# Half-height rows of a projection joined to a row-split matmul run, with the moves that go with it

## Chip, cores, metric

One core of one Trainium2 chip. The metric is the device time of one execution in microseconds, as the median of several runs; the profile gives the span of one execution, which is some 2 us shorter. Every profiled run told of here was in the fast state, with a granted TensorE clock of 0.998 or more, and the ratios use fast runs alone.

Abbreviations of the profile: PE is TensorE, DVE is VectorE, ACT is ScalarE, POOL is GpSimd, SPq is the queue of SyncE, which issues the DMAs here.

## The reference, cut to what matters

```python
# x: 1 x 2048 x 576, 32 heads of 18; feed-forward width 4608
h = layernorm(x) * (1 + ca) + sa
x = x + ga * (linear_attention(h) @ wo)          # the output projection
h = layernorm(x) * (1 + cb) + sb
x = x + gb * (relu(h @ w1) @ w2)                 # first and second feed-forward product
```

## The kernel before

The rows are 16 tiles of 128. After a first phase (keys, values, queries of all tiles, and tiles 0 and 1 up to the feed-forward input) come eight blocks. Block b does the feed-forward part of tiles 2b and 2b+1 and, in between, attention, projection and second layer norm of the next two tiles. The first product of a block (`l1`) has three groups; 576 is 4 x 128 + 64, so the last 64 rows are done as a pair of half-height matmuls, one in rows 0 to 63 of the array and one in rows 64 to 127, each in its own bank:

```python
def l1_rest(js, u, hb):
    for n, j in enumerate(js):
        for hf in range(2):
            b0 = 64 * hf
            pe.matmul(PS[:, 2 * u + hf, n * 256:n * 256 + 256], lhsT=w1b[b0:b0 + 64, j * P:(j + 1) * P],
                      rhs=hb[b0:b0 + 64, 4, :], start=False, stop=False, skip_group_check=True)
```

The output projection has the same 64 rows left, but does them as a full-array matmul with zeros:

```python
def wo_mm(t, pr, add_x):
    for k in range(2):
        if add_x:      # tiles 0 and 1: residual through an identity matmul
            pe.matmul(pr[:, k, 0:HD], lhsT=ident[:, 0:P], rhs=x_sb[:, t, k * HD:(k + 1) * HD], start=True, stop=False)
        for ci in range(NC):                        # NC = 5, the fifth is half empty
            pe.matmul(pr[:, k, 0:HD], lhsT=oT[:, t % 2, ci, :], rhs=wo_sb[:, ci, k * HD:(k + 1) * HD], ...)
```

What is called here as each block runs (shortened):

```python
def in_l1(g, u):                                    # during the first product
    if (g, u) in ((0, -1), (0, 1)):  q_fin(q); q_in(q + NL)      # query preparation of the next two tiles
    if (g, u) in ((1, 2), (2, 1)):   num_mm(t, pr); num_o(t, pr); turn_dma(oT[:, t % 2], o_sb[:, t % 2, :])
def in_l2(pos):                                     # during the second product, 14 positions of 9 matmuls
    if pos in (1, 4):  wo_mm(t, pr, False); <residual add>; bn(1, t)
    if pos in (2, 6):  ln2_rs(t); ln2_apply(t, None); turn_dma(h2...)
    if pos == 12:                                   # scale the normalised rows of both tiles, in place
        for ci in range(NC):
            dve.tensor_scalar(out=hb[:, ci, :], in0=hb[:, ci, :], scalar1=..., scalar2=..., op0=ALU.mult, op1=ALU.add)
```

Query preparation is a VectorE sum and reciprocal, a GpSimd multiply of 128 x 576 (L291), a transposing DMA, and a reload of the same buffer for a later tile, which must wait until that transpose has landed.

The softmax here doesn't subtract the row's maximum and nothing guards it: scores larger than these inputs give would overflow.

## Time and profile before

| | before |
|---|---|
| time | 393.02 us (391.85 to 393.25) |
| span, TensorE busy | 390.7 us, 98% |
| first phase, up to the first feed-forward matmul | 93.5 us |
| one block (blocks 0 to 6) | 37.05 us |
| block 7 and tail | 37.8 us |

The block lengths are distances between the starts of two first products in the timeline of TensorE, for instance 315.82 - 278.77. The view of waits shows none of TensorE in the blocks, so a block is all but the sum of its matmuls (a wait of 0.09 us that the view doesn't show comes up in experiment 7).

### The profile page before, as it was taken

How to read it: one execution, taken by the hardware profiler on the slowest of the kernel's cores; microseconds unless marked ns; L12 is line 12 of the kernel's file. 1: busy time of each engine (PE TensorE's matmuls, PEld its weight loads, DVE VectorE, ACT ScalarE, POOL GpSimd, SP SyncE). 2: the span in 40 equal slices, each digit the busy share in tenths (PEclk: the TensorE clock that was granted, in tenths of full speed). 3: DMA queues.
4: the chain of work that ended last, by engine and by line, in shares of the span. 5: the costliest groups of instructions: out<-in, count | busy, mean ns of one | idle time of the engine just before them, and what ended most of it. 6: DMA issues, size and time to landing. Idle time of an engine off the chain costs nothing.

```text
span 390.7 us, 8908 instructions
## 1 busy us (share of the span) xinstructions
PE 383.8 (98%) x3693; PEld 311.7 (80%) x3693; DVE 244.3 (63%) x452; ACT 157.9 (40%) x360; POOL 142.3 (36%) x199
## 2 busy tenths in 40 slices
PE   8999999999999999999999999999999999999995
PEld 4778888878887888788888878887888788878874
DVE  0889998854879746573755567458555664653221
ACT  1798779699531233124213510531143123312510
POOL 2155858741101510740164045306510641072045
PEclk9999999999999999999999999999999999999999
DMA  7999739795732151125313311450143124010001
GB/s 291 418 420 403 274 133 354 178 306 161 189 65 35 47 121 20 35 61 109 35 27 83 80 35 32 107 65 19 47 93 35 24 69 51 18 34 33 3 0 32
DMA packets 49515, 44.36 MB, mean 114 GB/s; under 512 B 39361, under 2 KB 42050, under 8 KB 48706
## 3 DMA queue, kind: packets, MB, share of 16 engines
q1 hardware_dynamic: 49186, 43.59, 39.6%
q8 instruction: 29, 0.48, 0.5%
q10 hardware_dynamic: 288, 0.19, 0.2%
q14 instruction: 12, 0.10, 0.1%
HBM read 27.97 MB, written 6.49 MB: 88 GB/s over the span
## 4 chain that ended last, share of the span: by engine, by line
PE 86%; POOL 6%; ACT 2%; DVE 2%; DMA 2%; issue 1%; SPq 0%; POOLq 0%; DVEq 0%; ACTq 0%
PE PS L683 33%; PE PS L742 29%; PE PS L274 9%; PE PS L410 5%; PE PS L690 5%; POOL wo_sb L637 2%; PE PS L235 2%; PE PS L391 1%; ACT RT L279 1%; POOL RH L754 1%; DMA gatd<-gt 1%; PE PS L324 1%; POOL RT L291 1%; DMA ga_row<-gatd 1%; DVE st L240 1%
## 5 line engine op out<-in xcount | busy, mean ns | idle before, releaser
L683 PE MATMUL PS<-h,R 128*128 128x256 bf16 x1152 | 133.5, 273 | 0.0
L683 PEld LDWEIGHTS <-R 128*128 128x128 bf16 x1152 | 109.8, 98 | 17.5 <-issue 5.1
L742 PEld LDWEIGHTS <-RH 128*128 128x128 f16 x864 | 84.5, 98 | 21.8
L728 POOL TENSOR_TENSOR yt<-yt,gb_row 128x288 f32<-128x288 f32 x23 | 16.8, 731 | 167.0 <-DVE yt L727 167.0
L742 PE MATMUL PS<-R,RH 128*128 128x288 bf16 (+1 forms) x576 | 75.6, 286 | 0.0
L697 ACT ACTIVATE RH<-PS 128x256 f16<-128x256 f32 x72 | 27.7, 384 | 114.0 <-PE PS L690 107.4
L699 DVE SCALAR_TENSOR_TENSOR RH<-PS,RH 128x256 f16<-128x256 f32 x72 | 30.1, 419 | 68.2 <-ACT RH L697 68.2
L279 ACT ACTIVATE RT<-PS,rs 128x576 bf16<-128x576 f32 x64 | 43.0, 750 | 7.5 <-PE PS L274 7.1
L698 ACT ACTIVATE RH<-PS 128x512 f16<-128x512 f32 x72 | 42.9, 595 | 7.8 <-PE PS L683 6.5
L746 ACT ACTIVATE RS<-PS 128x288 f32<-128x288 f32 x24 | 9.9, 411 | 75.9 <-PE PS L742 75.9
L742 PE MATMUL PS<-RT,RH 128*128 128x288 f16 x288 | 37.9, 286 | 0.0
L274 PE MATMUL PS<-RH,R 116*128 116x288 bf16 x240 | 31.8, 286 | 0.5 <-ACT RH L631 0.5
L754 POOL TENSOR_TENSOR RH<-RH,RT 128x2304 f16<-128x2304 f16 x7 | 31.8, 4548 | 0.0
L274 PE MATMUL PS<-RH,RT 116*128 116x288 bf16 x240 | 31.7, 286 | 0.0
L274 PEld LDWEIGHTS <-R 116*128 116x128 bf16 x240 | 22.9, 98 | 6.4 <-issue 0.7
L274 PEld LDWEIGHTS <-RT 116*128 116x128 bf16 x240 | 22.7, 98 | 5.5
L420 DVE TENSOR_SCALAR xn<-x_sb,mv,rs 128x576 bf16<-128x576 bf16 (+1 forms) x28 | 22.4, 842 | 7.3 <-ACT rs L415 7.3
L729 POOL TENSOR_TENSOR x_sb<-yt,x_sb 128x288 bf16<-128x288 f32 x31 | 22.8, 737 | 5.9 <-DVE yt L725 4.1
L240 DVE BATCH_NORM_STATS2 st<-x_sb 128x6 f32<-128x288 bf16 x60 | 24.2, 445 | 0.5
L410 PE MATMUL PS<-wo_sb,oT 128*128 128x288 bf16 x160 | 22.6, 286 | 0.2 <-POOL wo_sb L637 0.2
L284 DVE TENSOR_REDUCE Rk<-RT 128x64 f32<-128x1152 bf16 x16 | 21.2, 1332 | 1.4 <-ACT RT L279 1.4
L284 DVE TENSOR_REDUCE Rq<-RT 128x64 f32<-128x1152 bf16 x16 | 21.5, 1342 | 0.0
(115 smaller groups left out, 414.2 us busy)
## 6 DMA issues: line engine op xcount, KB each, us to landing
R<-in_w1a_dram SPq DMA_DIRECT2D x4, 1152.0 KB
eqd<-RT SPq DMA_DIRECT2D x14, 288.0 KB, 5.8
RT<-eqd SPq DMA_DIRECT2D x14, 288.0 KB, 2.7
R<-in_w2a_dram SPq DMA_DIRECT2D x3, 864.0 KB, 10.4
R<-in_w2b_dram SPq DMA_DIRECT2D x2, 1296.0 KB, 10.9
out_dram<-x_sb SPq DMA_DIRECT2D x15, 144.0 KB, 3.3
RT<-in_xT_dram SPq DMA_DIRECT2D x2, 640.0 KB
x_sb<-in_xk_dram SPq DMA_DIRECT2D x3, 288.0 KB
```

The source lines that it names most:

```text
L240: dve.bn_stats(out=s[:, hf, :], in_=x_sb[:, t, hf * HD:(hf + 1) * HD])
L274: pe.matmul(pr[:, k, 0:HD], lhsT=xt(t, ck), rhs=w[0:R, ck, k * HD:(k + 1) * HD], start=(ck == 0), stop=(ck == NC - 1))
L279: act.activation(out=E.rearrange("p (b h s e) -> p b h s e", b=2, s=2, e=DH)[:, :, :, s, :], in_=pr[:, :, 0:HD].rearrange("p b (h e) -> p ...
L284: dve.tensor_reduce(out=Rr, in_=E.rearrange("p (c e) -> p c e", e=DH), axis=AXX, op=ALU.add)
L410: pe.matmul(pr[:, k, 0:HD], lhsT=oT[:, t % 2, ci, :], rhs=wo_sb[:, ci, k * HD:(k + 1) * HD], start=(ci == 0 and not add_x), stop=(ci == NC ...
L683: pe.matmul(PS[:, 2 * u + hf, n * 256:n * 256 + 256], lhsT=w1a[:, ci, jj * P:(jj + 1) * P], rhs=hb[:, ci, :], start=(n == 0 and ci == 0), ...
L697: act.activation(out=A11[:, j, :], in_=lo[:, :, 0, :], func=ACT.Relu)
L698: act.activation(out=A2[:, j, :, :], in_=PS[:, 2 * u + 1, :].rearrange("p (n s f) -> p n s f", n=2, s=2), func=ACT.Relu)
L699: dve.scalar_tensor_tensor(out=U3[:, j, :], in0=lo[:, :, 1, :], scalar=0.0, in1=A11[:, j, :], op0=ALU.max, op1=ALU.subtract)
L729: pool.tensor_tensor(out=x_sb[:, t, c], in0=y, in1=x_sb[:, t, c], op=ALU.add)
L742: pe.matmul(PS[:, bank, 0:HD], lhsT=am[:, j, :], rhs=bm[:, j, :], start=first and j == 0, stop=(j % 9 == 8), skip_group_check=True)
L754: pool.tensor_tensor(out=A12, in0=A12, in1=U2, op=ALU.subtract)
```

## The change

The intent: TensorE is the bound, so take matmul time from it. From tile 6 on, the last 64 rows of the projection become a pair of half-height matmuls that joins an existing row-split run. For that the projection moves into the first product, attention ahead of it, and the query preparation back into the second product. Both halves of the array need the 64 rows, so the weights hold them twice and ScalarE copies 64 columns before the transpose (neither is in the cut diff). For tiles 0 and 1 VectorE adds the residual in place of four identity matmuls. The very last product is cut in two column halves in two banks, so that VectorE's work on the first half lies beside the second.

```diff
 # first phase, order of jobs (W projection, lb/lr/ap statistics, logarithm and exponential, scaling; eQ exponentials)
-Q9:1 eQ8 W0:3 eQ9 sq7 lb0 ot1:2 sq8 Q10:0 oc1 sq6 lr0 W1:1 ap0 eQ10 sq9 lb1 xc0 ht0:2 ...
+Q9:1 eQ8 W0:3 eQ9 sq7 xr0 lb0 ot1:2 sq8 Q10:0 oc1 sq6 lr0 W1:1 ap0 eQ10 sq9 xr1 lb1 ht0:2 ...
+    def add_res(t, pr):
+        x = v2(x_sb[:, t, :])
+        dve.tensor_tensor(out=x, in0=x, in1=pr[:, :, 0:HD], op=ALU.add)
 # [... cut: same for W, lb, ap without the identity matmul ...]
 # first product
             for u in range(3):
                 l1_rest(js[u], u, hb)
+            hooks(g, "rest")
 # blocks
+    def wo_rest(t, pr):
+        for k in range(2):
+            b0 = 64 * k
+            pe.matmul(pr[:, k, 0:HD], lhsT=oT[b0:b0 + 64, t % 2, 4, :], rhs=wo_sb[b0:b0 + 64, 4, k * HD:(k + 1) * HD],
+                      start=True, stop=False, skip_group_check=True)
+            # in_l1; blocks 0 and 1 stay much as they were [cut], and block 1 also does:
+                if b and (g, u) == (1, 0):
+                    q_next(t0 + 2)
+            # blocks 2 to 6:
+            if (g, u) in ((0, 0), (0, 2)):
+                attend(t0 + u // 2)
+            if g and u == "rest":
+                wo_rest(t0 + g - 1, pair(3))
+            if g and u == 0:
+                wo_full(t, pair(3)); add_res(t, pair(3)); bn(1, t)
+            if (g, u) == (1, 2):
+                norm2(b, t0)
+            # in_l2
+            if pos == (6 if b < 2 else 1):
+                norm2(b, t0 + 1)
+            if b > 1 and pos in (4, 9) or b == 1 and pos == 9:
+                q_next(t0 + 2 + pos // 9)
 # tail
+        for i, bank in enumerate((Z, 0)):
+            # [cut: 18 matmuls of 144 columns]
+            dve.tensor_tensor(out=yt[:, 0, c], in0=PS[:, bank, c], in1=gb_row[:, g], op=ALU.mult)
+            dve.tensor_tensor(out=x_sb[:, t, g], in0=yt[:, 0, c], in1=yl[:, c], op=ALU.add)
```

More of the change, by code (lines that the diff above doesn't have):

```diff
@@ L56 @@
 tp2 Q5:2 eQ4 sq3 tp1 wo3 nu0:3 eQ5 Q6:0 sq4 nO0 wo0 qi2 Q7:1 eQ6 wo1 sq5 ot0:2 w2b1 eQ7 nu1:3 Q8:0 nO1 oc0
-Q9:1 eQ8 W0:3 eQ9 sq7 lb0 ot1:2 sq8 Q10:0 oc1 sq6 lr0 W1:1 ap0 eQ10 sq9 lb1 xc0 ht0:2 sq10 Q11:0 ha0 hd0 lr1
-Q12:3 eQ11 ap1 Q13:2 qi3 xc1 eQ12 sq11 ht1:0 Q14:1 hd1 ha1 sq12 eQ13 Q15:3 qi4 eQ14 sq13 eQ15 sq14 sq15
+Q9:1 eQ8 W0:3 eQ9 sq7 xr0 lb0 ot1:2 sq8 Q10:0 oc1 sq6 lr0 W1:1 ap0 eQ10 sq9 xr1 lb1 ht0:2 sq10 Q11:0 ha0 hd0
+lr1 Q12:3 eQ11 ap1 Q13:2 qi3 eQ12 sq11 ht1:0 Q14:1 hd1 ha1 sq12 eQ13 Q15:3 qi4 eQ14 sq13 eQ15 sq14 sq15
 """
@@ L403, in turn_dma, with wo_mm @@
         sp.dma_start_transpose(dst, src.rearrange("p (c f) -> p c f", f=P))
-    def wo_mm(t, pr, add_x):
+    def wo_mm(t, pr):
         for k in range(2):
-            if add_x:
-                pe.matmul(pr[:, k, 0:HD], lhsT=ident[:, 0:P], rhs=x_sb[:, t, k * HD:(k + 1) * HD], start=True, stop=False)
             for ci in range(NC):
                 pe.matmul(pr[:, k, 0:HD], lhsT=oT[:, t % 2, ci, :], rhs=wo_sb[:, ci, k * HD:(k + 1) * HD],
-                          start=(ci == 0 and not add_x), stop=(ci == NC - 1))
+                          start=(ci == 0), stop=(ci == NC - 1))
+    def add_res(t, pr):
+        x = v2(x_sb[:, t, :])
+        dve.tensor_tensor(out=x, in0=x, in1=pr[:, :, 0:HD], op=ALU.add)
     def ln2_rs(t):
@@ L415, in ln2_rs, with ln2_apply @@
         act.activation(out=rs2[:, t, 0:1], in_=lnv[:, t:t + 1], func=ACT.Exp, scale=-0.5)
-    def ln2_apply(t, src):
+    def ln2_apply(t):
         def cols(o, i):
@@ L421, in cols @@
                               op0=ALU.subtract, op1=ALU.mult)
-        if src is None:
-            cols(xn[:, t % 2, 0:D], x_sb[:, t, :])
-            cols(xn[:, t % 2, D:640], x_sb[:, t, 512:D])
-        else:
-            cols(v2(xn[:, t % 2, 0:D]), src[:, :, 0:HD])
-            cols(xn[:, t % 2, D:640], src[:, 1, 224:HD])
+        cols(xn[:, t % 2, 0:D], x_sb[:, t, :])
+        cols(xn[:, t % 2, D:640], x_sb[:, t, 512:D])
     G5, FW = 504, 72
@@ L466, in tile_block @@
     SS = RS[:, 0:6 * HD].bitcast(FP32).rearrange("p (a f) -> p a f", f=HD)
+    yl = RE[:, 0:2 * HD].bitcast(FP32)
     X, Y, Z = 6, 4, 7
@@ L519, in wv_scale @@
             eng.tensor_scalar(out=o, in0=i, scalar1=f, scalar2=None, op0=ALU.mult)
-    def ln2_bn(i, pr):
-        for hf in range(2):
-            dve.bn_stats(out=st[:, i, hf, :], in_=pr[:, hf, 0:HD])
-        dve.bn_aggr(out=mv[:, 1, i, :], in_=st[:, i])
     def turn(src, pr):
@@ L642, in tile_block @@
         "oc": lambda i: act.activation(out=flat(oT[:, i]), in_=bf(at["ot", i][:, 0, :])[:, 0:640], func=ACT.Copy),
-        "W": lambda i: wo_mm(i, at["W", i], True), "lb": lambda i: ln2_bn(i, at["W", i]), "lr": ln2_rs,
-        "xc": lambda i: act.activation(out=v2(x_sb[:, i, :]), in_=at["W", i][:, :, 0:HD], func=ACT.Copy),
-        "ap": lambda i: ln2_apply(i, at["W", i]),
+        "W": lambda i: wo_mm(i, at["W", i]), "xr": lambda i: add_res(i, at["W", i]), "lb": lambda i: bn(1, i), "lr": ln2_rs,
+        "ap": lambda i: ln2_apply(i),
         "ht": lambda i: turn2(xn[:, i, :], at["ht", i]),
@@ L763, in l2 @@
         fin(t + 1, 1, Z, 2)
+        H4 = HD // 2
+        if b + 1 == NB:
+            dve.tensor_tensor(out=yl[:, H4:HD], in0=PS[:, Z, H4:HD], in1=SS[:, 1, H4:HD], op=ALU.add)
+            dve.tensor_copy(out=yl[:, 0:H4], in_=SS[:, 1, 0:H4])
+            pool.tensor_tensor(out=yl, in0=yl, in1=gb_row[:, HD:D], op=ALU.mult)
+            pool.tensor_tensor(out=yl, in0=yl, in1=x_sb[:, t, HD:D], op=ALU.add)
         prod(X, A22, T4, al)
@@ L771, in l2, with q_next, attend, wo_full @@
             return
-        rows, z = slice(t * P, (t + 1) * P), yt[:, 1, :]
+        rows = slice(t * P, (t + 1) * P)
         sp.dma_start(outf[rows, 0:HD], x_sb[:, t, 0:HD])
-        pool.tensor_tensor(out=z, in0=SS[:, 1, :], in1=gb_row[:, HD:D], op=ALU.mult)
-        pool.tensor_tensor(out=z, in0=z, in1=x_sb[:, t, HD:D], op=ALU.add)
-        prod(Z, A12, B22, al)
-        dve.tensor_tensor(out=yt[:, 0, :], in0=PS[:, Z, 0:HD], in1=gb_row[:, HD:D], op=ALU.mult)
-        dve.tensor_tensor(out=x_sb[:, t, HD:D], in0=yt[:, 0, :], in1=z, op=ALU.add)
+        for i, bank in enumerate((Z, 0)):
+            c, g = slice(i * H4, (i + 1) * H4), slice(HD + i * H4, HD + (i + 1) * H4)
+            for j in al:
+                pe.matmul(PS[:, bank, c], lhsT=A12[:, j, :], rhs=B22[:, j, c], start=(i == 1 and j == 0),
+                          stop=(j == NK - 1), skip_group_check=True)
+            dve.tensor_tensor(out=yt[:, 0, c], in0=PS[:, bank, c], in1=gb_row[:, g], op=ALU.mult)
+            dve.tensor_tensor(out=x_sb[:, t, g], in0=yt[:, 0, c], in1=yl[:, c], op=ALU.add)
         sp.dma_start(outf[rows, HD:D], x_sb[:, t, HD:D])
     NB = NT // 2
+    def q_next(q):
+        if q < NT:
+            q_fin(q)
+            if q + NL < NT:
+                q_in(q + NL)
+    def attend(t):
+        pr = pair(3)
+        num_mm(t, pr)
+        num_o(t, pr)
+        if t > 5:
+            act.activation(out=o_sb[:, t % 2, D:640], in_=o_sb[:, t % 2, 512:D], func=ACT.Copy)
+        turn_dma(oT[:, t % 2], o_sb[:, t % 2, :])
+    def wo_rest(t, pr):
[3 more added lines that the diff above has]
+                      start=True, stop=False, skip_group_check=True)
+    def wo_full(t, pr):
+        for k in range(2):
+            for ci in range(4):
+                pe.matmul(pr[:, k, 0:HD], lhsT=oT[:, t % 2, ci, :], rhs=wo_sb[:, ci, k * HD:(k + 1) * HD],
+                          start=False, stop=(ci == 3), skip_group_check=True)
+    def norm2(b, t):
+        ln2_rs(t)
+        ln2_apply(t)
+        i = t % 2
+        turn_dma(h2[:, (b + 1) % 2, :, i * P:(i + 1) * P], xn[:, i, :])
     for b in range(NB):
@@ L788, in in_l1 @@
                 return
-            if (g, u) in ((0, -1), (0, 1)):
-                q = t0 + max(u, 0)
-                q_fin(q)
-                if q + NL < NT:
-                    q_in(q + NL)
-            if (g, u) in ((1, 2), (2, 1)):
-                t = t0 + g - 1
-                pr = pair(3)
-                num_mm(t, pr)
-                num_o(t, pr)
-                turn_dma(oT[:, t % 2], o_sb[:, t % 2, :])
+            if b < 2:
+                if (g, u) in ((0, -1), (0, 1)):
+                    q_next(t0 + max(u, 0))
+                if (g, u) in ((1, 2), (2, 1)):
+                    attend(t0 + g - 1)
+                if b and (g, u) == (1, 0):
+                    q_next(t0 + 2)
+                return
+            if (g, u) in ((0, 0), (0, 2)):
[3 more added lines that the diff above has]
+            if g and u == 0:
+                t = t0 + g - 1
+                wo_full(t, pair(3))
+                add_res(t, pair(3))
+                bn(1, t)
+            if (g, u) == (1, 2):
+                norm2(b, t0)
         def in_l2(pos):
@@ L803, in in_l2 @@
                 return
-            if pos in (1, 4):
+            if b < 2 and pos in (1, 4):
                 i = pos // 4
-                t = t0 + i
-                pr = pair(i)
-                wo_mm(t, pr, False)
-                dve.tensor_tensor(out=v2(x_sb[:, t, :]), in0=v2(x_sb[:, t, :]), in1=pr[:, :, 0:HD], op=ALU.add)
-                bn(1, t)
-            if pos in (2, 6):
-                i = pos // 4
-                t = t0 + i
-                ln2_rs(t)
-                ln2_apply(t, None)
-                turn_dma(h2[:, (b + 1) % 2, :, i * P:(i + 1) * P], xn[:, t % 2, :])
+                wo_mm(t0 + i, pair(i))
+                add_res(t0 + i, pair(i))
+                bn(1, t0 + i)
+            if b < 2 and pos == 2:
+                norm2(b, t0)
+            if pos == (6 if b < 2 else 1):
+                norm2(b, t0 + 1)
+            if b > 1 and pos in (4, 9) or b == 1 and pos == 9:
+                q_next(t0 + 2 + pos // 9)
             if pos == 12:
@@ L901, in _layout @@
     wo[:D] = g["A_wo"]
+    wo[D:] = g["A_wo"][512:]
     o["wo"] = flat(wo.reshape(NC, P, D).transpose(1, 0, 2))
```

## The prediction

> **What bounds the kernel now.** I read the head of the page first, then the waits of TensorE, then the chain of waits in order of time for one block of two row tiles, then the timelines of the two places outside the steady blocks that the change touches: the start of the output projection and the tail.
>
> ```profile
> PE 383.8 (98%) x3693; PEld 311.7 (80%) x3693; DVE 244.3 (63%) x452; ACT 157.9 (40%) x360; POOL 142.3 (36%) x199
> ...
> PE PS L410 <- POOL wo_sb L637: 0.2, 1, 0.2
> ```
>
> TensorE is busy 98% of the span, and its waits add up to 3.0 us in five places. The one shown, 0.2 us, is in code that the change touches; the other four are in the first 26 us. So time is won only by taking TensorE work away, and lost wherever TensorE is made to wait. Block 5 in the chain (start, duration, what):
>
> ```profile
> 288.10 0.76 PE PS L690 x12
> ...
> 299.20 1.23 PE PS L410 x10
> 300.43 3.31 PE PS L742 x27
> 303.73 1.23 PE PS L410 x10
> 304.96 11.03 PE PS L742 x90
> ```
>
> The chain through a block is TensorE alone. A 288-column full-array matmul costs 11.03/90 = 0.1226 us, and the projection's ten cost the same each (1.23). A row-split run of twelve 256-column matmuls takes 0.76; twelve full ones would take 12 x 0.109 = 1.31 (28 in 3.06 elsewhere in the chain). Six pairs side by side are 0.66, so 0.10 of the run is entering and leaving the split.
>
> The start of the projection, TensorE, VectorE and ScalarE timelines (start, duration):
>
> ```profile
> 85.48 0.78 PE L410 MATMUL PS<-wo_sb,oT 128*128 128x288 bf16 x5
> ...
> 86.83 0.44 PE L535 MATMUL PS<-ident,xn 128*128 128x128 bf16 x5
> 87.11 3.84 PE L274 MATMUL PS<-RH,RT 116*128 116x288 bf16 x30
> ```
> ```profile
> 84.05 0.47 DVE L523 BATCH_NORM_STATS2 st<-PS 128x6 f32<-128x288 f32 x1 [0.27 <-PE PS L410]
> 84.55 0.21 DVE L524 BATCH_NORM_AGGREGATE mv<-st 128x2 f32<-128x12 f32 x1
> 85.48 1.13 DVE L420 TENSOR_SCALAR xn<-PS,mv,rs 128x576 bf16<-128x576 f32 x2 [0.72 <-ACT rs L415]
> ```
> ```profile
> 84.93 0.28 ACT L414 ACTIVATE lnv<-mv,eps_t 128x1 f32<-128x1 f32 x1
> ...
> 85.56 1.37 ACT L279 ACTIVATE RT<-PS,rs 128x576 bf16<-128x576 f32 x2
> ```
>
> See how close it is: the normalised tile is ready at 85.48 + 1.13 = 86.61 and the transposes that read it start at 86.83; the exponentials that free the banks of the next query product end at 86.93 and that product starts at 87.11. Each has only 0.2 us to spare. Later, on VectorE and ScalarE, the same residual-and-statistics sequence as the change will use here:
>
> ```profile
> 300.46 0.76 DVE L809 TENSOR_TENSOR x_sb<-x_sb,PS 128x576 bf16<-128x576 bf16 x1 [1.23 <-PE PS L410]
> 301.25 0.82 DVE L240 BATCH_NORM_STATS2 st<-x_sb 128x6 f32<-128x288 bf16 x2
> 302.11 0.21 DVE L241 BATCH_NORM_AGGREGATE mv<-st 128x2 f32<-128x12 f32 x1
> ...
> 302.35 0.29 ACT L414 ACTIVATE lnv<-mv,eps_t 128x1 f32<-128x1 f32 x1 [0.38 <-DVE mv L241]
> ```
>
> From the add to the logarithm is 302.35 - 300.46 = 1.89 us. The tail:
>
> ```profile
> 385.23 0.73 POOL L729 TENSOR_TENSOR x_sb<-yt,x_sb 128x288 bf16<-128x288 f32 x1 [0.64 <-DVE yt L725]
> ...
> 386.73 0.73 POOL L775 TENSOR_TENSOR yt<-yt,x_sb 128x288 f32<-128x288 f32 x1
> 386.89 0.46 DVE L777 TENSOR_TENSOR yt<-PS,gb_row 128x288 f32<-128x288 f32 x1 [1.75 <-PE PS L742]
> 387.49 0.46 DVE L778 TENSOR_TENSOR x_sb<-yt 128x288 bf16<-128x288 f32 x1
> 387.98 0.33 SPq L779 DMA_DIRECT2D out_dram<-x_sb  x1
> ```
>
> GpSimd (ends 387.46) and TensorE (386.79, then VectorE) reach the last add nearly together; then the last store goes out at 387.98 and 2.7 us of transfer and closing follow.
>
> **What the Trainium skill says.** "TensorEngine Tiling (Array Packing)", section Key Properties: changing the tiling mode drains the array, tiles within a mode run in parallel. The trace agrees: 0.76 us for a run, with 0.10 for both ends by the working above. "TensorE: Matmul & The Clock Gate", section Back-to-back issue gap: N/2.4 + 2.5 ns, which for 288 columns is 122.5 ns; the trace has 122.6. "PSUM — Partial Sum Buffer", section Engine vs sequencer instructions: the queues of ScalarE, VectorE and GpSimd are strict first in, first out; the timelines agree, as every engine keeps program order. "SBUF — State Buffer", section Who interferes with whom: VectorE in a two-port mode and GpSimd exclude each other. The trace shows it: the pair of scalings at L420 that began at 308.06, beside the 4.55 us GpSimd subtraction, took 2.89 us against 0.64 for the pair at 303.45 before it.
>
> **Part 1, half-height rows joined to the row-split run.** Only from tile 6 on (blocks 2 to 6 prepare tiles 6 to 15): ten tiles. Each had ten full matmuls; now eight full and one pair of 64-row matmuls, directly behind an existing row-split run in another pair of banks, so no additional mode change. Saved per tile: 2 x 0.1226 - 0.1226 = 0.123; ten tiles: **-1.23 us**, all on TensorE's path, if nothing waits.
>
> **Part 2, the moves that go with it.** Attention of the next two tiles moves to the first group of the feed-forward product, the projection to its second and third, and the query preparation back into the preceding second product. I walked a block, with 0 at the end of the first row-split run. First attention: TensorE 0 to 0.38, VectorE done about 1.6, the new 64-column ScalarE copy about 1.9, the transposing DMA lands about 2.6 later (median to landing), so 4.5; the joined matmuls come at 0.38 + 0.87 + 1.31 + 0.38 + 3.06 + 0.76 = 6.8. Second attention's bank pair is read by about 5.5, also before 6.8. The second tile's residual add ends some 1.2 us before the second product takes its bank. In that product (0 at its start), GpSimd subtracts until about 11.1 and the operand is needed at 12 x 1.1 = 13.2; the query transpose lands about 16 and is needed at 15.4 + 3.8 = 19.3. No wait, so **0**. One exception, block 1: there a third query preparation stands in the DMA-issuing queue ahead of a projection transpose, and its following reload must wait for its landing; I get that transpose landing at 9.9 to 10.3 against a need at 10.1: **+0.1**.
>
> **Part 3, residual by VectorE for tiles 0 and 1.** Removed: four identity matmuls, 0.123 each. The first tile's first one only shortens the way to the existing wait for the scaled weights (until 82.63), so 3 x 0.123 = 0.37 earlier: the transposes could start at 86.83 - 0.37 = 86.46. But VectorE now adds before it takes statistics. Projection end: 84.02 - 0.12 = 83.90; add at 83.93; logarithm at 83.93 + 1.89 = 85.82 instead of 84.93; ScalarE done with both small functions at about 86.35; scaling from bf16 0.64 instead of 1.13, ends 87.0. So TensorE waits from 86.46 to 87.05. In ScalarE's queue the exponentials stand behind those small functions: 86.35 + 1.37 = 87.7, and the next query product starts at 87.7 instead of 87.11. After that I find slack: the following products' banks are free in time, the second tile's normalised rows (90.3) precede their transposes (91.4). Sum: **+0.6**, a loss where the removed matmuls promised -0.37. The two removed ScalarE copies were off the path.
>
> **Part 4, the last product in two banks.** 36 matmuls of 144 columns at 62.5 ns (estimate from the skill's formula) against 18 of 0.1226: 2.25 against 2.21, +0.04. The VectorE multiply and add behind the last matmul shrink from 0.46 each to some 0.3 each (estimate: half the columns, the rest fixed), and GpSimd's part is done earlier: last data at 387.6 instead of 387.95. But GpSimd now does its two extra operations before the other tile's last add, which moves from 385.23 to about 386.2; that tile's store is issued at 387.0, another at 387.4, and the last can only be issued at 387.8. **-0.15**.
>
> Sum: -1.23 + 0 + 0.1 + 0.6 - 0.15 = -0.7, so 393.0 - 0.7 = 392.3. As I may have been too severe in part 3, I say 392.2.
>
> **Rivals.** (a) Part 3 pays as intended: if the add hides, -0.37 instead of +0.6, and the time is 391.4. Against it stand the two margins of 0.2 us and an added operation of 0.76 that only a 0.49 faster scaling makes up, and that not for ScalarE. (b) A new wait in every block, by a transposing DMA that lands late (its worst was 4.3 instead of 2.6) or by ScalarE standing at its copy for VectorE while the rectifications queue: 0.5 us in five blocks is +2.5, so 394.8. For it: DMA order in one queue is strict; against: the walk leaves about 1 us or more. (c) The pair doesn't overlap, or the longer run costs more: part 1 gives about 0, and the time is 393.5. The twelve in 0.76 speak against it. (d) The tail gives its full 0.35 or more: 392.0. To move 2%, 7.9 us, in either direction, none of these is enough.
>
> **Range.** The three runs of before spread over 1.4 us, more than the effect. With (a) and (d) as the low side and part of (b) as the high: 390.9 to 393.6. Faster by over 2%: 0.01; within: 0.98; slower: 0.01.
>
> **What would show it.** Right: row-split runs of 14 in blocks 2 to 6, some 0.12 longer than those of 12, no TensorE wait beside them, and blocks about 0.25 shorter (37.05 to 36.8); a wait near 87 for the scaling or the exponentials, and the first feed-forward product at about 94.1 instead of 93.52. Last store issued within 1.1 us after the last matmul, with the three stores back to back. Wrong: the first product starting at or before 93.5 (then part 3 fails), a wait at the joined matmuls for a DMA (part 2), or 14-matmul runs of 1.0 us (part 1).

## More of the kernel before

One more view matters, and the prediction doesn't show it: the end of a second product, VectorE and GpSimd (start, duration, engine, line, form, count).

```profile
314.26 1.78 DVE L820 TENSOR_SCALAR h<-h,mod 128x256 bf16<-128x256 bf16 x5
...
314.42 0.77 POOL L729 TENSOR_TENSOR x_sb<-yt,x_sb 128x288 bf16<-128x288 f32 x1 [0.64 <-DVE yt L725]
```

The five scalings that the next block's matmuls read take 1.78 us, with one GpSimd operation beside them, and end at 316.04. The next block's matmuls have begun at 315.82 on the first parts; the fourth matmul needs the fourth scaling.

## The result, and the profile after

The changed kernel is correct and takes 396.14 us (395.76 to 396.28, 4 runs) against 392.51 for the kernel before in the same rounds. The ratio is 1.009, with a 95% interval of 1.0067 to 1.0114. Ratios here are the mean time of one kernel's fast runs over that of the other's of the same rounds, so not quite the ratio of the medians. It is a loss of 3.6 us clear of noise, and outside the range of the prediction.

The head of the page and the waits of TensorE after (line waiting, tile and line waited for; us in total, times, longest):

```profile
PE 383.6 (97%) x3706; PEld 310.7 (79%) x3707; DVE 237.8 (60%) x458; ACT 156.6 (40%) x368; POOL 139.3 (35%) x199
```
```profile
PE PS L676 <- DVE h L862: 2.4, 6, 0.4
...
PE PS L408 <- DMA oT<-o_sb: 0.6, 1, 0.6
...
PE PS L274 <- ACT RT L279: 0.3, 1, 0.3
...
PE PS L529 <- DVE xn L422: 0.2, 1, 0.2
```

L862 is the scaling (L820 before); L676 is the first product. There are six new waits at the starts of blocks 2 to 6 (two of them in block 3), one for an attention transpose, and two in the first phase. Block 7 starts without one; in block 6 there are no queries left to prepare. A wait is counted from the modelled end of the matmul before it, so the delay of the stream is longer than the number: in block 5 three matmuls start at 281.58 and the fourth, which should come at 281.58 + 3 x 0.109 = 281.91, starts at 282.66, so 0.75 us late.

Block 5 in the chain of waits (start, duration, what):

```profile
280.02 1.79 DVE h L862 x3
281.85 0.78 DVE h L862
282.66 2.89 PE PS L676 x25
...
292.42 0.76 PE PS L683 x12
293.30 1.09 PE PS L809 x8
```

Before, this chain was TensorE alone; now it goes through the scalings. The joined pair is in the gap between the last two lines; the timeline has the run of 14 from 292.35 to 293.23, 0.88 us, against 0.76 for one of 12.

The same stretch on VectorE and GpSimd, which answers to the view of 314 to 316 of the kernel before:

```profile
280.02 2.85 DVE L862 TENSOR_SCALAR h<-h,mod 128x256 bf16<-128x256 bf16 x5
...
279.18 1.17 POOL L291 TENSOR_TENSOR RT<-RT,ratq 128x576 bf16<-128x576 bf16 x1
280.31 0.73 POOL L722 TENSOR_TENSOR yt<-yt,gb_row 128x288 f32<-128x288 f32 x1
281.11 1.41 POOL L723 TENSOR_TENSOR x_sb<-yt,x_sb 128x288 bf16<-128x288 f32 x2
```

The scalings start as early as before (1.56 us ahead of the next first product in both), but take 2.85 us instead of 1.78. GpSimd, which had one operation there, now has four, as the query multiplies before them have pushed the rest back. VectorE isn't idle: each scaling is recorded as longer.

The first phase, TensorE and ScalarE:

```profile
86.61 0.45 PE L529 MATMUL PS<-ident,xn 128*128 128x128 bf16 x5 [0.24 <-DVE xn L422]
87.41 3.83 PE L274 MATMUL PS<-RH,RT 116*128 116x288 bf16 x30 [0.34 <-ACT RT L279]
...
86.00 1.35 ACT L279 ACTIVATE RT<-PS,rs 128x576 bf16<-128x576 f32 x2
```

The two waits are where the prediction put them: the query product at 87.41 begins when the exponentials end, 86.00 + 1.35 = 87.35. This run's stream is 0.25 us ahead at the first projection (81.78 against 82.03), and 0.29 us behind at the first feed-forward matmul (93.81 against 93.52).

The tail, TensorE, GpSimd, VectorE, and the last store:

```profile
388.07 2.41 PE L777 MATMUL PS<-R,RH 128*128 128x144 bf16 x36
...
389.69 0.73 POOL L723 TENSOR_TENSOR x_sb<-yt,x_sb 128x288 bf16<-128x288 f32 x1
...
390.46 0.31 DVE L779 TENSOR_TENSOR yt<-PS,gb_row 128x144 f32<-128x144 f32 x1 [1.67 <-POOL x_sb L723]
...
391.70 0.33 SPq L781 DMA_DIRECT2D out_dram<-x_sb  x1
```

The first half's matmuls end about 389.2, but VectorE's multiply of that half starts at 390.46, when GpSimd has let go of the scratch half that both use. From the start of the last product to the last store it is 3.63 us; before it was 387.98 - 384.42 = 3.56.

Where the 3.7 us of the span (394.4 - 390.7) came from, by starts in the timeline of TensorE:

| stretch | before | after | difference |
|---|---|---|---|
| to the first feed-forward matmul | 93.52 | 93.81 | +0.29 |
| block 0 | 37.05 | 37.05 | 0 |
| block 1 | 37.05 | 37.85 | +0.80 |
| blocks 2 to 6 | 185.25 | 187.80 | +2.55 |
| block 7 and tail | 37.83 | 37.89 | +0.06 |

### The profile page after: what moved, and what is told of

It is laid out like the page before. It is cut to its first block, busy times and chain, and to the rows that moved or that the text cites. A ratio compares the mean times of both kernels' runs of the same rounds, so it can differ in the third digit from the quotient of the medians.

```text
span 394.4 us, 8939 instructions
## 1 busy us (share of the span) xinstructions
PE 383.6 (97%) x3706; PEld 310.7 (79%) x3707; DVE 237.8 (60%) x458; ACT 156.6 (40%) x368; POOL 139.3 (35%) x199
## 4 chain that ended last, share of the span: by engine, by line
PE 79%; DVE 6%; POOL 5%; DMA 4%; ACT 3%; issue 2%; SPq 0%; POOLq 0%; DVEq 0%; ACTq 0%
PE PS L676 32%; PE PS L736 24%; PE PS L274 8%; PE PS L683 5%; DVE h L862 3%; PE PS L809 3%; POOL wo_sb L631 2%; PE PS L408 2%; PE PS L235 2%; ACT RT L279 1%; PE PS L391 1%; POOL RH L748 1%; DMA gatd<-gt 1%; DMA h<-xn 1%; DVE st L240 1%
## 5 line engine op out<-in xcount | busy, mean ns | idle before, releaser
L676 PE MATMUL PS<-h,R 128*128 128x256 bf16 x1152 | 134.3, 273 | 2.5 <-DVE h L862 2.4
L676 PEld LDWEIGHTS <-R 128*128 128x128 bf16 x1152 | 111.0, 98 | 19.2 <-issue 6.3
L736 PEld LDWEIGHTS <-RH 128*128 128x128 f16 x846 | 82.8, 98 | 20.8
L736 PE MATMUL PS<-R,RH 128*128 128x288 bf16 (+1 forms) x558 | 72.4, 286 | 0.0
L692 DVE SCALAR_TENSOR_TENSOR RH<-PS,RH 128x256 f16<-128x256 f32 x72 | 28.8, 413 | 63.7 <-ACT RH L690 63.7
L721 DVE TENSOR_TENSOR yt<-PS,RS 128x288 f32<-128x288 f32 x23 | 10.4, 452 | 29.7 <-POOL RH L748 21.0
L240 DVE BATCH_NORM_STATS2 st<-x_sb 128x6 f32<-128x288 bf16 x64 | 25.8, 446 | 0.6
L413 DVE TENSOR_TENSOR x_sb<-x_sb,PS 128x576 bf16<-128x576 bf16 x16 | 12.0, 753 | 13.9 <-PE PS L809 8.1
```

Source lines behind the costliest of these rows:

```text
L240: dve.bn_stats(out=s[:, hf, :], in_=x_sb[:, t, hf * HD:(hf + 1) * HD])
L676: pe.matmul(PS[:, 2 * u + hf, n * 256:n * 256 + 256], lhsT=w1a[:, ci, jj * P:(jj + 1) * P], rhs=hb[:, ci, :], start=(n == 0 and ci == 0), ...
L692: dve.scalar_tensor_tensor(out=U3[:, j, :], in0=lo[:, :, 1, :], scalar=0.0, in1=A11[:, j, :], op0=ALU.max, op1=ALU.subtract)
L736: pe.matmul(PS[:, bank, 0:HD], lhsT=am[:, j, :], rhs=bm[:, j, :], start=first and j == 0, stop=(j % 9 == 8), skip_group_check=True)
```

## The experiments

Two theories for the blocks. **L (port lock)**: VectorE's scalings and GpSimd exclude each other, and the moved query multiplies bring GpSimd's work beside them. **D (late data)**: the rows reach the scaling late because projection, residual add and the second transposing DMA have moved. For the start of block 5 the changed kernel's own trace already speaks against D: the second tile's transposing DMA is issued 11.9 us before the scalings start at 280.02, and such a DMA lands 2.6 us after its issue in the median.

```profile
268.11 1.20 SPq L403 DMA_TRANSPOSE h<-xn  x1
```

Times of the kernel before in the rounds: 392.21 for the first four runs, 392.23 for the next four, 392.24 for the last.

**1. Query preparation moved back into the first product.**

```diff
+            if g < 2 and u == -1:
+                q_next(t0 + 2 + g)
             if (g, u) in ((0, 0), (0, 2)):
                 attend(t0 + u // 2)
-            if b > 1 and pos in (4, 9) or b == 1 and pos == 9:
+            if b == 1 and pos == 9:
```

> Changed kernel, with the two query preparations of blocks 2 to 6 taken out of the second product and put at the start of the first and second group of the first product, where GpSimd is idle. Theory L (port lock): in the changed kernel the five scalings of the normalised rows on VectorE (L862, median 0.644 us against 0.335 before) stand beside GpSimd's query multiplies and wait for them, and that holds the first matmuls of the next block 0.75 us; so here the scalings return to about 1.8 us for five, the wait at the start of blocks 3 to 6 goes, block time falls from 37.5 to about 36.8, and the time is 396.1 - 4 x 0.75 = about 393.1. Theory D (late data): the scalings are late because of the moved projection, residual add and second transposing DMA; then nothing changes at the block starts and the time stays within 0.5 us of 396.1.

Measured: 394.23 us (393.58 to 394.57), ratio 1.0051 (1.0031 to 1.0071). In the view of one line's instructions (duration in ns, minimum, median, maximum) the scalings are short again; the first line is from the kernel before, the second from the changed one, the third from this one:

```profile
L820 DVE TENSOR_SCALAR h<-h,mod x35: 330/335/768, 129.0 to 352.8; 128x256 bf16<-128x256 bf16 x35
```
```profile
L862 DVE TENSOR_SCALAR h<-h,mod x35: 332/644/886, 129.3 to 356.4; 128x256 bf16<-128x256 bf16 x35
```
```profile
L864 DVE TENSOR_SCALAR h<-h,mod x35: 333/338/843, 129.3 to 354.6; 128x256 bf16<-128x256 bf16 x35
```

The wait at the starts of blocks 3 to 6 is gone, and blocks 5 and 6 take 36.71 us (318.21 - 281.50 and 354.93 - 318.21 in the chain). D, which expected no change, fails for these blocks. The time fell by 1.9 us, not 3: new waits on attention transposes in blocks 2 to 4 took the rest back (block 2 is 38.54 us long against 37.57), and that of block 1 stayed. From the view of waits of TensorE:

```profile
PE PS L803 <- DMA oT<-o_sb: 1.0, 2, 0.8
```

**2. GpSimd work added to the kernel before.**

```diff
+            if pos == 11:
+                for _ in range(2):
+                    pool.tensor_tensor(out=dum[:], in0=dum[:], in1=dum[:], op=ALU.mult)
             if pos == 12:
```

> Kernel before, with two added GpSimd multiplies of 128x576 bf16 on a scratch tile (as large as the query multiply) between GpSimd's last two pairs of operations in the second product of blocks 0 to 6; nothing reads their result. Theory L: VectorE's scalings (L820) are held by them, the five take over 2.8 us instead of 1.8, and the first product of the next block starts 0.7 to 1.1 us late, seven times: 5 to 8 us longer than before. Theory D: no engine on the path gets more work, so the time stays within 0.5 us of before.

Measured: 400.72 us (400.52 to 401.58), ratio 1.0223 (1.0202 to 1.0244), 8.5 us longer. Nothing reads the added result, no matmul was added, and yet a block takes 38.10 us (259.29 - 221.19 between second groups) against 37.05. Its scalings, and the waits of TensorE for them:

```profile
L825 DVE TENSOR_SCALAR h<-h,mod x35: 332/719/1304, 128.5 to 361.0; 128x256 bf16<-128x256 bf16 x35
```
```profile
PE PS L685 <- DVE h L825: 5.2, 14, 1.0
```

This shows L in the other direction: GpSimd work beside the scalings is enough, without any part of the change, to make TensorE wait. The loss came out just above the expected 5 to 8 us.

**3. The scalings on ScalarE.**

```diff
-                    dve.tensor_scalar(out=hb[:, ci, :], in0=hb[:, ci, :], scalar1=mod2[:, 1, ci:ci + 1],
-                                      scalar2=mod2[:, 0, ci:ci + 1], op0=ALU.mult, op1=ALU.add)
+                    act.activation(out=hb[:, ci, :], in_=hb[:, ci, :], func=ACT.Identity, scale=mod2[:, 1, ci:ci + 1],
+                                   bias=mod2[:, 0, ci:ci + 1])
```

> Changed kernel, with the five scalings per block done by ScalarE instead of VectorE at the same place in the program. Theory L: [...]the wait at the start of blocks 2 to 7 goes and the time is 396.1 - 3.7 = about 392.4. Theory D: the rows come late for any engine; the wait stays and the time is within 1 us of 396.1.

Measured: 394.87 us (393.9 to 395.06), ratio 1.0071 (1.005 to 1.0092). Blocks 4 to 6 take 36.7 us with no wait, as L expects. But the total missed by 2.5 us. The profiled run, the fastest of the four, shows waits in blocks 1 to 3 for DMA transposes (1.1 and 0.6 us for attention, 0.5 for a query) and 0.4 us for the scalings at the start of block 2, where the second tile's rows did land late. (The expectation speaks of blocks 2 to 7; the changed kernel has these waits in blocks 2 to 6.) ScalarE began the scalings 5.0 us before the first product of each of blocks 3 to 7, where VectorE had begun 1.56 us before; so the rows were there early, which speaks against D at these starts too. Each scaling took 0.58 to 0.60 us on ScalarE, with GpSimd at work beside them. As they also ran earlier, this run shows less of the lock itself than runs 1 and 2.

**4. Only the residual by VectorE.** The kernel before, with part 3 of the change alone (order of jobs, `add_res`, statistics and scaling from SBUF).

> Kernel before, with only part 3 of the change (residual by VectorE for tiles 0 and 1, no identity matmuls). By the working of the prediction a loss of 0.55 us: a wait of some 0.2 us at the transposes and 0.3 us at the next query product, and the first feed-forward product 0.5 to 0.6 us later. Rival: the part is neutral or gains 0.37 us and the whole loss of the change lies in the blocks.

Measured: 392.45 us against 392.21, ratio 1.0008 (0.9985 to 1.003). In time alone that doesn't tell a loss of 0.5 us from none. The trace does: its first phase is the same as that of the changed kernel within 0.01 us, with a wait of 0.24 us at 86.61 and of 0.35 us at 87.41, and first feed-forward matmul at 93.81. From the first projection matmul (82.03 before, 81.78 here) that is 12.03 us against 11.49, so 0.54 us more. The rival, a neutral or gaining part, falls by the trace. The other traces agree: where the projection doesn't wait for the scaled weights, the stretch is 11.14 us with the identity matmuls (runs 2, `final_full`, `final2`) and 11.57 without (runs 3 and 5), so the part costs 0.43 to 0.54 us.

**5. Query preparation cut in two.** Run 1 left waits on attention transposes. In block 1 of the changed kernel the queue of DMA issues has (start, duration):

```profile
144.64 1.64 SPq L350 DMA_TRANSPOSE RE<-RT  x1
148.24 0.32 SPq L339 DMA_DIRECT2D RT<-eqd  x1
148.66 2.61 SPq L403 DMA_TRANSPOSE oT<-o_sb  x2
```

The reload L339 waits 3.6 us for the landing of the transpose before it, and the attention transpose L403, whose data VectorE had ready at 144.8, can only follow. The Trainium skill's page "DMA: Bandwidth & Descriptors", section Anatomy of one DMA — SWDGE (gpsimd) path, says, of DMAs that GpSimd issues, that the wait for a semaphore happens on the issuing sequencer, before the DMA is handed on. Here SyncE issues, and these lines show the same: nothing is issued for 2 us until the reload goes out at 148.24. The cut leaves the VectorE and GpSimd half early and puts the DMA half behind the attention transposes:

```diff
+    def q_work(q):
+        q_sm(q); q_pool(q)
+    def q_move(q):
+        q_turn(q); q_in(q + NL)                     # limits on q left out
+            # block 1: q_work(t0 + 1 + g) at (1, 0) and (2, 0); both q_move at (2, 2)
+            # blocks 2 to 6: q_work(t0 + 2 + g) at (0, -1) and (1, -1); both q_move at pos 2 of the second product
```

> Changed kernel, with the query preparation cut in two: VectorE's sums and GpSimd's multiply at the start of the first and second group of the first product (blocks 2 to 6; in block 1 in its second and third group), and the transposing DMA and the reload after it in the second product (in block 1 after the last attention transpose). Theory Q: what is left in the run with whole preparations moved (0.7 to 0.8 us waits for the attention transposes in blocks 1 and 2, 0.2 in block 3) comes from the queue that issues the DMAs, where a reload waits for the landing of the transpose before it and holds the attention transpose behind it. Then all waits on attention transposes go, and the time is 396.1 - 3.7 - 0.8 = about 391.6. Rival: the transposes are slow for the traffic of other transfers; then waits of 0.5 us or more on them stay in blocks 1 to 3 and the time is about 393.

Measured: 392.0 us (391.57 to 392.15), ratio 0.9993 (0.998 to 1.0007). No wait on an attention transpose is left in the trace, so the order of the queue was the cause. One wait of 0.8 us is left in block 1, now for VectorE (experiment 8), so that block still takes 37.92 us, and the time is 0.4 above the expected 391.6. All of the change but the other waits in the blocks is still in this kernel, and it stands level with the kernel before.

**6. Another scratch half in the tail.** `yt[:, 0, c]` becomes `yt[:, 1, c]` in the last two lines of the diff above.

> Changed kernel, with the products of the last two half-banks written to the other half of the scratch tile. In the changed kernel the first half's multiply (ready when its 18 matmuls end, about 1.1 us before the second's) began only when GpSimd had read the same scratch half for the other tile, at 390.46. Theory B: that reuse set the end; here the first multiply starts within 0.2 us of the end of its matmuls, and the last store is issued about 0.9 us after the last matmul instead of 1.4: 0.4 us off the span behind the last matmul, 395.7 in time. Rival: the order of the three stores sets it, then less than 0.15 us.

Measured: 396.12 us, in time no difference to the changed kernel (396.14, of other rounds), at a size that the rounds don't resolve. The trace shows it:

```profile
389.43 0.31 DVE L779 TENSOR_TENSOR yt<-PS,gb_row 128x144 f32<-128x144 f32 x1 [0.67 <-PE PS L777]
...
391.33 0.40 SPq L781 DMA_DIRECT2D out_dram<-x_sb  x1
```

The multiply starts 1 us earlier, and from the start of the last product to the last store it is 391.33 - 388.04 = 3.29 us instead of 3.63. Behind the end of the last matmul the span is 0.26 us shorter (3.67 against 3.93), where 0.4 was expected. The reuse of the scratch half had set the end; what remains is the order of the stores, issued at 390.43, 390.81 and 391.33.

**7. Everything put together, and the same without the joined rows.** `final` keeps the joined rows and the cut query preparation, keeps the identity matmuls, and in the tail uses the other scratch half and lets VectorE do the other tile's last add. `final_full` is the same with ten full matmuls per tile.

> Version from the findings: identity matmuls kept for tiles 0 and 1, query preparation in halves, last product in two banks with its own scratch half and the other tile's last add on VectorE, joined rows kept. Blocks 3 to 6 take 36.7 us as in the run with preparations moved, the first feed-forward product starts as early as before, the last store is issued 0.9 us after the last matmul. 1.2 us from the joined rows and 0.35 from the tail: about 1.5 us under the kernel before, ratio 0.996.

Measured: 390.84 us (390.35 to 391.18), ratio 0.9965 (0.9953 to 0.9978), as expected. Start of the last product to last store: 386.35 - 383.21 = 3.14 us.

> As final, but the projection's last rows stay full-array matmuls (ten per tile, no joined pair, no ScalarE copy). Theory of part 1: 0.123 us more per tile for ten tiles, 1.2 us longer than final, blocks 3 to 6 at about 36.95. Rival: the pair in the split run is worth nothing (it runs one after the other), then the same as final within 0.3 us.

Measured: 391.95 us (391.6 to 392.5), ratio 0.9995 (0.9983 to 1.0008). The joined rows are worth 1.1 us in time; blocks take 36.96 instead of 36.71, which is 0.25 us for two tiles. So the pair does overlap. The 36.96 is 0.09 under the 37.05 of before; with all matmuls kept, that came with the moves. The trace of the kernel before shows where:

```profile
297.12 0.76 DVE L399 TENSOR_TENSOR o_sb<-PS,rden 128x576 bf16<-128x576 f32 x1
...
297.94 1.26 PE L742 MATMUL PS<-R,RH 128*128 128x288 bf16 x9
```

In each of blocks 0 to 6 the first matmul of the second product started 0.20 us after the matmul ahead of it instead of 0.11. It writes the bank that VectorE's attention division (L399, ends at 297.88) reads last. From block 2 on, attention now comes two groups earlier, and the step is 0.11, as it is in block 7 of the kernel before, which has no attention. The view of waits counts from the modelled end of the matmul ahead, which lies later, so it lists no wait here.

**8. Order of VectorE in block 1.** `final` had one wait left in the blocks, of my own making:

```profile
PE PS L749 <- DVE o_sb L399: 0.8, 1, 0.8
```

```diff
-                if b and g and u == 0:
-                    q_work(t0 + 1 + g)
+                if b and (g, u) == (1, 0):
+                    q_work(t0 + 2)
                 if b and (g, u) == (2, 2):
+                    q_work(t0 + 3)
```

> As final, with block 1's second query sum put behind the attention division of its second tile on VectorE. In final that sum stood ahead of the division, which frees the bank that the next product writes, and TensorE waited 0.8 us there once (L749, released by VectorE's L399). If VectorE's order was the cause, the wait goes and the time falls by 0.8 to about 390.0, ratio to before 0.9945; if the bank is late for another reason, it stays and the time stays at 390.8.

Measured: 390.49 us (389.79 to 390.7), ratio 0.9952 (0.9938 to 0.9965). The wait is gone, and block 1 takes 37.05 instead of 37.92. In time only 0.35 us of it shows, between two sets of rounds. This is the fastest version: 1.75 us under the kernel before.

## Why the prediction was wrong

The size and the sign were wrong: 392.2 in a range of 390.9 to 393.6, against 396.14.

**The step that failed is part 2, "No wait, so 0".** The walk checked when data and banks would be ready, and that GpSimd's subtraction and the query transposes would be in time; in blocks 3 to 6 those held. What it left out was the length of the five scalings at the end of the second product. They were taken as they had been, while GpSimd's four operations moved beside them. From 1.78 us for five they became 2.85, and the fourth matmul of each next block came 0.75 us late or more. The prediction had quoted the lock, and its trace sign (2.89 against 0.64 us), but applied it to no operation of the changed schedule. In numbers: blocks of 36.71 without the wait would have given 5 x (37.05 - 36.71) = 1.70 us less for blocks 2 to 6; they took 2.55 more, so waits at their starts cost 4.25 us. Runs 1 and 2 show from both sides that GpSimd's work beside the scalings is the cause; that a shared port is the mechanism isn't shown, as no run here tells it from another lock between the two engines. Of these 4.25 us, the part at the start of block 2 had a second cause, rows that landed late after block 1; the two weren't separated there. The 0 also missed a gain: the hidden wait of 0.09 us per block (experiment 7) went with the moves, so time was to be won without taking matmuls away.

**The exception in block 1 had the right mechanism and the wrong size.** The queue did hold the attention transpose behind a reload: +0.1 was predicted, +0.80 measured. The landing of the query transpose took 3.6 us instead of the median 3.2, and the attention transpose behind it 3.2 instead of 2.6; I had taken medians for both.

**Part 1 was right.** The run of 14 took 0.88 us, 0.12 more than the run of 12, and the comparison of `final` with `final_full` gives 0.25 us per two tiles, as worked out. Its 0.10 for both ends of a split run was misread, though without effect here, as the pair joins a run: the 0.76 goes from the start of the first pair to the start of the next full matmul, so it holds the leaving alone. Entering costs another 0.10, in the step ahead of the run (0.205 us instead of 0.109).

**Part 3 was right** in place, cause and size: both waits, and 0.54 us of loss on the stretch against 0.6 predicted. The wait at the transposes was 0.24 us instead of the 0.59 worked out, as they began after the first of the two scalings (ended 86.56); the product behind them came where it was put.

**Part 4 was mis-sized**: -0.15 predicted, +0.06 measured. The working had the other tile's last add later on GpSimd and the stores queued behind each other, but it missed that the first half's multiply writes the scratch half that this add reads. With that taken away (run 6), 0.34 us came back.

**Rival (b)** of the prediction, a new wait in every block, named the right form, but not the place or the size: 0.5 us in five blocks and 394.8, against 0.85 a block (4.25 us in five) and 396.14. It looked for the wait at the joined matmuls, for DMA or for ScalarE. The range took in only a part even of that.

## What to carry to other kernels

When work moves between stages on a side engine, list for each place what will now run beside it, and look for instructions there that grow longer beside it; the length of such an instruction isn't a constant of the kernel. A blocked VectorE instruction shows here as a longer one (up to 0.89 us instead of 0.33), not as idle time, so compare the median and maximum of one line's durations between two traces before looking for late data. And keep a DMA that must wait (a reload of a buffer in use) behind the urgent ones in its queue; cutting a helper into its compute half and its DMA half was enough here.

## What the Trainium skill lacked or had wrong

- "SBUF — State Buffer", section Who interferes with whom, says of VectorE in a two-port mode and GpSimd that whoever issues first has the shared port pair for the whole instruction and the other blocks. The traces agree, and add what a row of short VectorE instructions does: they take turns with GpSimd. Five scalings of 0.33 us beside four GpSimd operations took 2.85 us, about one scaling for each GpSimd operation, with a median of 0.644 us; with two added multiplies of 1.15 us in front, the median was 0.719 and the longest 1.304.
- "TensorEngine Tiling (Array Packing)", section Key Properties, says that a change of tiling mode drains the array, with no figure. Here entering a row-split run of 256-column matmuls cost 0.10 us (0.205 from start to start instead of 0.109) and leaving it another 0.10 (0.202 instead of 0.106), and one more pair inside a run 0.12 us for 288 columns.
- "DMA: Bandwidth & Descriptors" has no time for a transposing DMA of a tile of this size on this chip (the one in "VectorE: DVE Perf Modes", section The three transpose paths, is for a single 128 x 128 tile). Here one takes 1.20 to 1.30 us of the issuing queue as a rule, and from issue to landing 2.6 us (five 128-column parts, longest 4.3) or 3.2 us (nine parts, longest 4.7) in the median.
